# Two levels of Strassen's algorithm for the output product of a fused attention and feed-forward kernel

## The chip, the cores and the metric

The kernel runs on one core of one Trainium2 chip. The metric is the device time of one execution in microseconds (us), the median over several runs. Engines are named as in the profile: PE is the matmul engine, PEld its loading of the stationary operand, DVE the vector engine, ACT the scalar engine, POOL the GpSimd engine, SP the queue that issues most transfers.

## What is computed

Attention with a hash mask, then a feed-forward block with a quick GELU, all in float32 (the two weight matrices arrive as float64). Cut to what matters:

```python
batch, n_heads, seq, head_dim = (4, 8, 768, 64)          # attention, q k v in float32
mask = q_bucket[:, :, :, None] == k_bucket[:, :, None, :] # 6 sign bits of a projection
attn = softmax(where(mask, q @ k.T / sqrt(D), -1e9));  x = attn @ v
x = x.transpose(0, 2, 1, 3).reshape(3072, 512)            # tokens x d_model
h = x @ w_in                                              # 512 x 2048, float64 weights
g = h * (1.0 / (1.0 + np.exp(-1.702 * h)))
out = (g @ w_out).astype(np.float32)                      # 2048 x 512, float64 weights
```

## The kernel before

The attention part (up to about 334 us of the profile) leaves x transposed in on-chip memory (`xT`, model dimension on partitions, 3072 tokens along the free axis). The change does not touch it. What follows is `feed_forward`, in two stages.

**Hidden stage.** The hidden product is made by one level of Strassen's algorithm (in the variant with seven products and fifteen sums). There are 24 tasks: three blocks `sb` of 1024 tokens, and in each eight tasks `mt` of 2 x 128 hidden units. A task is a 2 x 2 block product: the two halves of the hidden units (i), the two halves of the model dimension (summed over), the two 512-token halves of the block (j). `hidden(sb, mt)` supplies the matmuls of one product: two steps of the inner dimension, 128 x 128 stationary, 512 streamed. The profile shows a float32 matmul as two instructions ("passes"), so a product is 4 passes and a task 28. `task` runs the seven products in the order 1, 6, 7, 5, 2, 3, 4 and combines them: ACT copies product 1 out of PSUM, DVE makes seven adds, each of a PSUM tile and an SBUF tile of 128 x 512. The four finished quarters go through GELU on ACT and are stored to a scratch tensor in DRAM (`g_dram`).

The sums of weight quarters that Strassen's algorithm needs are made by POOL, one task ahead, in the first token block (`in_sums`, by way of `sums_a`, lines 198 to 201). The sums of activation quarters `xT` are made by DVE, once per token block (`sums_b`, lines 206 to 209).

Behind the adds of each task, work that isn't urgent is handed out from the list `todo`: the conversion of the float64 bits of one chunk of weights to float32 (`convert`, seven DVE instructions of 512 elements, lines 171 to 186, and one on ACT; two late chunks of `w_in` in tasks 1 and 2, then 16 chunks of `w_out`), and after these the sums of quarters of `w_out` (`sums_b` on POOL, four instructions of 2048 elements).

**Output stage.** Six tasks, one per 512 tokens, again one level of Strassen's algorithm over token halves, the halves of the 2048 hidden units and the halves of the 512 model dimensions. `fetch(n)` brings the four quarters of the hidden values back from `g_dram` (four transfers of 1 MB), `g_sums` makes the sums of quarters on DVE (four instructions of 2048 elements) while the task before is running, `outputs` has the hidden values as the stationary operand (128 x 128) and the weights or their sums streamed (256): 16 matmuls per product, 32 passes. The quarters come out with tokens on partitions and are stored directly.

**Order.** The instructions of PE, DVE, ACT and POOL run in the order of the program text (`manual_schedule`), each engine its own queue, in order. The transfers of SP are ordered by a planner from its own estimate of when each becomes possible, and are issued in that order. PSUM has eight banks, used in rotation by the products, so PE can be up to eight products ahead of the engine that empties them. The tiles `u`, `v`, `c12`, `c21`, `c22` of a task have two buffers each.

Of the kernel before, what the change touches and what calls it, by code (L numbers as in the profile page):

```python
# [19 lines left out]
P = 128  # L20
# [18 lines left out]
def kernel(  # L39
# [102 lines left out]
    g_dram = dram.tile([FC, P, N], F32, name="g_dram")  # L142
# [14 lines left out]
    def convert(cv, dst, src, queue=None):  # L157
# [4 lines left out]
        def of(x):  # L162
            return x if len(dst.shape) == 2 else x.rearrange("p (j d) -> p j d", j=dst.shape[1])
# [47 lines left out]
    K2, F2, D2 = KC // 2, FF // 2, DM // 2  # L211
# [448 lines left out]
    def feed_forward(tag, late=()):  # L660

        G2 = XT // 2
        outv = out.rearrange("(s i m p) (j d) -> s i j p m d", i=2, m=G2 // P, p=P, j=2)
        n1, n2 = N // (2 * XT), N // XT
        with ExitStack() as fctx:
            stage = fctx.enter_context(tc.tile_pool(name=f"stage{tag}", bufs=2, side="right"))
            late, todo_sums = list(late), []
            sets = [fctx.enter_context(tc.tile_pool(name=f"f0{tag}", bufs=6, space=PSUM, side="right"))]
            todo, turn = [], [-1]

            def task(mm, emit, mid=(), end=(), parts=1):
                u, v, c12, c21, c22 = (stage.tile([P, XT], F32, tag=x, name=x) for x in ("u", "v", "c12", "c21", "c22"))

                def product(i):
                    turn[0] += 1
                    ps = sets[turn[0] % 8 // 6 if len(sets) > 1 else 0].tile([P, XT], F32, tag="p", name="product")
                    mm(i, ps)
                    return ps

# [5 lines left out]
                emit(1, 1, c22)  # L685
                nc.vector.tensor_tensor(c12, p, v, op=Alu.add)
                nc.vector.tensor_tensor(u, product(2), u, op=Alu.add)
                emit(0, 0, u)
# [3 lines left out]
                emit(0, 1, c12)  # L692
                p = product(4)
                for cols in (slice(i * XT // parts, (i + 1) * XT // parts) for i in range(parts)):
                    nc.vector.tensor_tensor(c21[:, cols], p[:, cols], c21[:, cols], op=Alu.add)
                    emit(1, 0, c21[:, cols], cols.start)
                for x in end:
                    x()
                if todo:
                    todo.pop(0)()  # L700


            LEFT = dict(zip(range(1, 8), (0, 1, 6, 3, 4, 5, 2)))
            RIGHT = dict(zip(range(1, 8), (0, 2, 3, 6, 4, 5, 1)))

            def hidden(sb, mt):
                wq, xq = quarters_in(slice(mt * P, (mt + 1) * P)), quarters_x(sb)

                def mm(i, ps):
                    for kc in range(K2):  # L710
                        nc.tensor.matmul(ps, wq[LEFT[i]][:, kc, :], xq[RIGHT[i]][:, kc, :],  # L711
                                         start=(kc == 0), stop=(kc == K2 - 1))

                def emit(i, j, c, _=0):
                    nc.scalar.activation(c, c, Act.Gelu_apprx_sigmoid)  # L715
                    t0 = (2 * sb + j) * XT
                    loader[0].dma_start(out=g_dram[i * (FC // 2) + mt, :, t0 : t0 + XT], in_=c)

                steps = sums_b(nc.vector, *quarters_x(sb + 1)) if mt == FC // 2 - 1 and sb + 1 < n1 else []
                return mm, emit, steps[:3], steps[3:]  # L720
# [3 lines left out]
            def g_views(n):  # L724

                if n % 2:
                    x = [w_in_sb[:, i, :].rearrange("p (c t) -> p c t", t=G2) for i in range(4)]
                    return x + [s_in[:, i].rearrange("p k (c t) -> p k c t", t=G2) for i in range(3)]
                x = [xT[:, i, 0 : 4 * XT].rearrange("p (c t) -> p c t", t=G2) for i in range(4)]
                y = [xT[:, K2 * i : K2 * (i + 1), 4 * XT : 6 * XT].rearrange("p k (c t) -> p k c t", t=G2) for i in range(2)]  # L730
                z = t_x.rearrange("p i k t -> p (i k t)")[:, 0 : FC // 2 * G2].rearrange("p (k c t) -> p k c t", k=K2, t=G2)
                return x + y + [z]

            def fetch(n):
                for x, (i, k) in zip(g_views(n), ((0, 0), (0, 1), (1, 0), (1, 1))):
                    t0 = n * XT + i * G2
                    src = g_dram[k * (FC // 2) : (k + 1) * (FC // 2), :, t0 : t0 + G2].rearrange("c p t -> p c t")
                    loader[0].dma_start(out=x, in_=src)

            def g_sums(n):  # L740
                q = g_views(n)
                return sums_a(nc.vector, *[x.rearrange("p (k c) t -> p k c t", k=K2) for x in q[:4]], *q[4:])

            def outputs(n):
                gq = g_views(n)

                def mm(i, ps):
                    ps = ps.rearrange("p (m d) -> p m d", d=D2)
                    for m in range(G2 // P):
                        for c in range(FC // 2):  # L750
                            at = LEFT[i]
                            x = gq[at][:, c] if at < 4 else gq[at][:, c // (FC // 4), c % (FC // 4)]
                            nc.tensor.matmul(ps[:, m, :], x[:, m * P : (m + 1) * P], wqs[RIGHT[i]][:, c, :],  # L753
                                             start=(c == 0), stop=(c == FC // 2 - 1))

                def emit(i, j, c, start=0):
                    c = c.rearrange("p (m d) -> p m d", d=D2)
                    m0 = start // D2
                    loader[0].dma_start(out=outv[n, i, j][:, m0 : m0 + c.shape[1], :], in_=c)

                return mm, emit
# [12 lines left out]

            for sb in range(n1):
                for mt in range(FC // 2):
                    n = sb * (FC // 2) + mt
                    if n == 1:
                        wop = fctx.enter_context(tc.tile_pool(name=f"wo{tag}", bufs=1))
                        cv = fctx.enter_context(tc.tile_pool(name=f"cv{tag}", bufs=1))  # L780
                        w_out_sb = wop.tile([P, 2, FC, D2], F32, name="w_out_sb")
                        t_out = wop.tile([P, 3, FC // 2, D2], F32, name="t_out")
                        wqs += [w_out_sb[:, j, FC // 2 * k : FC // 2 * (k + 1), :] for k in range(2) for j in range(2)]
                        wqs += [t_out[:, i] for i in range(3)]
                        steps = conversions(cv, late + [(w_out_sb[:, :, fc, :], wo[fc]) for fc in range(FC)])
                        todo += [lambda: [next(steps) for _ in range(LATE)]] * 2 if late else []
                        todo += [lambda: (next(steps), next(steps))] * FC
                        todo += sums_b(nc.gpsimd, *wqs)
# [3 lines left out]
                    if (sb, mt) == (n1 - 1, 0):  # L792
                        fetch(0)
# [4 lines left out]
                    if sb == 0 and mt + 1 < FC // 2:  # L798
                        todo_sums = in_sums(mt + 1)
# [63 lines left out]
```

## Time and profile before

| | |
|---|---|
| time, median of 3 runs | 921.9 us (921.57 to 922.57) |
| the profiled execution | 921.21 us, span 919.2 us, mean granted PE clock 0.999 |
| PE busy in the span | 909.3 us (99%) |
| DVE, ACT, POOL busy | 569.8, 301.3, 157.3 us |
| attention | to about 334 us |
| hidden stage (matmuls of line 711) | 334.1 to 623.5 us |
| output stage (matmuls of line 753) | 623.5 to 913.6 us |
| DMA traffic | 94.2 MB, mean 102 GB/s |

All times of instructions are in microseconds from the start of the span. A line of a timeline gives the start, the duration, the engine, the line of the kernel, the operation, the output and inputs by the program's names, the output's and inputs' shapes, and in brackets how long the engine was idle before it and who released it. Matmul durations include the pipeline's fill and drain, so two matmuls in a row overlap; their pace is read from the chain of waits, which counts each microsecond once. In a group's row, behind the count: busy time, mean nanoseconds of one, idle time before, and what ended it.

### The profile page before, as it was taken

The page shows a single profiled execution, that of the slowest core. Times are in us where ns is not written, and L with a number is a line of the kernel's source. Part 1 is how long each engine was busy: PE and PEld are TensorE (multiplying, and loading weights), DVE is VectorE, ACT ScalarE, POOL GpSimd, SP SyncE. Part 2 cuts the span into 40 slices and gives each one's busy share as a digit, 9 for nine tenths or more (in the row PEclk, how much of TensorE's full clock was granted, in tenths as well). Part 3 has the DMA queues.
Part 4 walks back from the last instruction along what each step waited for, and adds up shares of the span by engine and source line. Part 5 has one row for each costly group of instructions (what it writes and reads, how often), then busy time and mean ns, then how long its engine had stood idle before and what let it go on. Part 6 is the DMA issues. An engine that isn't in the chain of part 4 may idle for free.

```text
span 919.2 us, 11502 instructions
## 1 busy us (share of the span) xinstructions
PE 909.3 (99%) x4245; PEld 536.3 (58%) x4245; DVE 569.8 (62%) x766; ACT 301.3 (33%) x483; POOL 157.3 (17%) x154
## 2 busy tenths in 40 slices
PE   9999999999999999999999999999999999999997
PEld 4444444444444444444444444448888888888886
DVE  4798888888889846788877888334413223141410
ACT  5656766765676532233333232221000000000000
POOL 4232432243333270500010002300000000000000
PEclk9999999999999999999999999999999999999999
DMA  4634345434433012343333572236333324140101
GB/s 100 119 80 101 79 85 101 102 81 83 97 78 79 21 35 103 116 153 120 138 138 126 186 260 108 88 129 226 115 115 115 115 85 145 58 125 12 35 13 36
DMA packets 171503, 94.21 MB, mean 102 GB/s; under 512 B 122128, under 2 KB 155056, under 8 KB 171440
## 3 DMA queue, kind: packets, MB, share of 16 engines
q1 hardware_dynamic: 170832, 92.45, 35.3%
q10 hardware_dynamic: 608, 0.96, 0.3%
q8 instruction: 35, 0.57, 0.3%
q14 instruction: 28, 0.23, 0.1%
HBM read 60.82 MB, written 31.46 MB: 100 GB/s over the span
## 4 chain that ended last, share of the span: by engine, by line
PE 97%; DVE 1%; DMA 1%; ACTq 0%; issue 0%; SPq 0%; ACT 0%; DVEq 0%
PE product L753 32%; PE product L711 31%; PE ps L419 16%; PE av L443 13%; PE dn L462 3%; PE hash L395 1%; DMA q<-in_q_dram 0%; PE tp L353 0%; ACTq L407 0%; PE warm L346 0%; PE hash L360 0%; DVE acc L435 0%; SPq L315 0%; DMA qf<-f 0%; DVE qT L378 0%
## 5 line engine op out<-in xcount | busy, mean ns | idle before, releaser
L420 ACT ACTIVATE e<-ps 128x768 f32<-128x768 f32 x192 | 151.4, 812 | 19.2 <-PE ps L419 13.1
L419 PE MATMUL ps<-qT,kT 64*128 64x384 f32 x768 | 155.1, 482 | 0.0
L711 PE MATMUL product<-xT,w_in_sb 128*128 128x512 f32 x288 | 135.5, 593 | 0.0
L443 PE MATMUL av<-e,v 128*64 128x385 f32 x768 | 130.2, 486 | 0.9 <-ACT xT L456 0.9
L715 ACT ACTIVATE c<-c 128x512 f32<-128x512 f32 x72 | 45.2, 630 | 183.9 <-DVE c L684 133.4
L680 ACT COPY u<-product 128x512 f32<-128x512 f32 x30 | 17.2, 575 | 246.0 <-PE product L753 242.0
L443 PEld LDWEIGHTS av<-e,v 128*64 128x64 f32 x768 | 54.9, 136 | 70.6 <-issue 69.0
L711 PEld LDWEIGHTS product<-xT,w_in_sb 128*128 128x128 f32 x288 | 54.6, 190 | 68.5 <-issue 60.7
L711 PE MATMUL product<-t_x,s_in 128*128 128x512 f32 x192 | 90.2, 592 | 0.0
L419 PEld LDWEIGHTS ps<-qT,kT 64*128 64x128 f32 x768 | 68.2, 188 | 35.5 <-issue 35.5
L427 POOL TENSOR_TENSOR acc<-e 128x768 f32<-128x768 f32 x32 | 49.3, 1542 | 208.1 <-DVE acc L435 139.6
L681 DVE TENSOR_TENSOR v<-product,u 128x512 f32<-128x512 f32 x30 | 20.6, 686 | 88.4 <-PE product L753 72.3
L419 PE MATMUL ps<-qf,kf 64*128 64x384 bf16 x384 | 63.0, 324 | 0.7 <-ACT e L420 0.6
L753 PE MATMUL product<-w_out_sb,xT 128*128 128x256 f32 x288 | 63.6, 379 | 0.0
L753 PE MATMUL product<-t_out,xT 128*128 128x256 f32 x288 | 63.6, 379 | 0.0
L753 PE MATMUL product<-w_out_sb,w_in_sb 128*128 128x256 f32 x288 | 63.6, 379 | 0.0
L711 PEld LDWEIGHTS product<-t_x,s_in 128*128 128x128 f32 x192 | 36.5, 190 | 45.9 <-issue 45.7
L753 PEld LDWEIGHTS product<-w_out_sb,xT 128*128 128x128 f32 x288 | 54.7, 190 | 7.9 <-issue 0.5
L753 PEld LDWEIGHTS product<-t_out,xT 128*128 128x128 f32 x288 | 54.7, 190 | 7.4
L753 PEld LDWEIGHTS product<-w_out_sb,w_in_sb 128*128 128x128 f32 x288 | 54.7, 190 | 7.4
L428 POOL TENSOR_TENSOR acc<-acc,e 128x768 f32<-128x768 f32 x32 | 56.7, 1773 | 2.5
L684 DVE TENSOR_TENSOR c<-product,c 128x512 f32<-128x512 f32 x30 | 20.7, 691 | 45.1 <-PE product L753 37.3
(127 smaller groups left out, 1125.9 us busy)
## 6 DMA issues: line engine op xcount, KB each, us to landing
g_dram<-c SPq DMA_DIRECT2D x72, 256.0 KB
xT<-g_dram SPq DMA_DIRECT2D x12, 1024.0 KB
w_in_sb<-g_dram SPq DMA_DIRECT2D x12, 1024.0 KB
raw<-in_moe_w_out_dram SPq DMA_DIRECT2D x16, 512.0 KB
raw<-in_moe_w_in_dram SPq DMA_DIRECT2D x15, 512.0 KB
v<-in_v_dram SPq DMA_DIRECT2D x32, 192.0 KB
g_dram<-u SPq DMA_DIRECT2D x24, 256.0 KB
k<-in_k_dram SPq DMA_DIRECT2D x60, 96.0 KB
```

The source lines that it names most:

```text
L419: nc.tensor.matmul(ps[:, j, 0:HS], a[hs, keys], m[hs, cols], start=not last, stop=last)
L420: nc.scalar.activation(es[c][:, kt, :, 0:HS], ps[:, :, 0:HS], Act.Exp, scale=1.0 / D**0.5)
L427: nc.gpsimd.tensor_tensor(acc, es[c][:, 0, :, 0:HS], es[c][:, 1, :, 0:HS], op=Alu.add)
L428: nc.gpsimd.tensor_tensor(acc, acc, es[c][:, 2, :, 0:HS], op=Alu.add)
L443: nc.tensor.matmul(av[D * j : D * (j + 1), :], vt[:, t, j, :], es[c][:, t, j, :], start=(t == 0), stop=(t == T - 1))
L462: nc.tensor.matmul(dn[D * j : D * (j + 1), :], ones, acc[:, j, :], start=True, stop=True)
L680: nc.scalar.copy(u, product(1))
L681: nc.vector.tensor_tensor(v, product(6), u, op=Alu.add)
L684: nc.vector.tensor_tensor(c22, p, c21, op=Alu.add)
L711: nc.tensor.matmul(ps, wq[LEFT[i]][:, kc, :], xq[RIGHT[i]][:, kc, :], start=(kc == 0), stop=(kc == K2 - 1))
L715: nc.scalar.activation(c, c, Act.Gelu_apprx_sigmoid)
L753: nc.tensor.matmul(ps[:, m, :], x[:, m * P : (m + 1) * P], wqs[RIGHT[i]][:, c, :], start=(c == 0), stop=(c == FC // 2 - 1))
```

## The change

The output product gets a second level: two levels of Strassen's algorithm in place of one.

- The hidden stage's task (now inside `hidden`) no longer stores only the four quarters of the hidden values. As soon as the quarters of a task have gone through GELU, POOL makes the four first-level sums of them (`sums_b` on POOL, 128 x 512 each, two of the results in place), and all seven first-level operands that the outer products need are stored to `g_dram`, whose layout now has partitions in front and rows of 2 KB per task. `in_sums` of the next task stand ahead of a task on POOL instead of behind it.
- The output stage has 21 steps: three token blocks of 1024, times seven outer products in the order 1, 6, 7, 5, 2, 3, 4. A step is again a Strassen product with seven inner products (order 1, 2, 3, 6, 7, 5, 4). Now the weights are the stationary operand (128 x 128) and the hidden values are streamed (256 tokens): an inner product is four matmuls.
- Before a step, its first-level operand is fetched in two transfers of 1 MB into one of two buffers, one step ahead, and DVE makes its four second-level sums (`sums_b`, 1024 elements). The first-level sums of `w_out` are made by DVE (2048 elements, behind tasks 21 and 22), the second-level ones by POOL (`sums_a`, 512 elements: four for the first step behind task 22, then four in each of the first six steps).
- The result of an outer product is accumulated while the inner products are combined: most steps add the four quarters of an earlier outer product, in SBUF, on DVE.
- Results have the model dimension on partitions. DVE turns them by 32 x 32 transposes (`turned`, four of 256 elements for each outer quarter), and they are stored in rows of 512 bytes (`written`).
- The conversion writes the columns of `w_out` split by their remainder modulo 4, a strided write.

The diff, cut:

```diff
-    g_dram = dram.tile([FC, P, N], F32, name="g_dram")
+    g_dram = dram.tile([7 * (N // 1024), P, FC // 2, 512], F32, name="g_dram")
...
-            return x if len(dst.shape) == 2 else x.rearrange("p (j d) -> p j d", j=dst.shape[1])
+            return x if len(dst.shape) == 2 else x.rearrange("p (x r) -> p x r", r=dst.shape[2])
...
+            def hidden(sb, mt, mid=(), end=()):
                 u, v, c12, c21, c22 = (stage.tile([P, XT], F32, tag=x, name=x) for x in ("u", "v", "c12", "c21", "c22"))
+                t2, t4 = (stage.tile([P, XT], F32, tag=x, name=x, bufs=1) for x in ("t2", "t4"))
...
+                def keep(at, x):
+                    loader[0].dma_start(out=g_dram[len(LEFT) * sb + at, :, mt, :], in_=x)
+
+                def emit(c, at=None):
+                    nc.scalar.activation(c, c, Act.Gelu_apprx_sigmoid)
+                    if at is not None:
+                        keep(at, c)
...
+                for f, kept in zip(sums_b(nc.gpsimd, u, c12, c21, c22, v, t2, t4), ((4, v), (1, c12), (5, t2), (6, t4))):
+                    f()
+                    keep(*kept)
                 for x in end:
                     x()
...
+            steps_out = [(sb, o) for sb in range(n1) for o in OUTER]
+            raw_g = [None, s_in[:, 0:2].rearrange("p i k f -> p (i k f)").rearrange("p (c t) -> p c t", t=XT)]
             def fetch(n):
+                sb, o = steps_out[n]
+                for h in range(2):
+                    cs = slice(h * F4, (h + 1) * F4)
+                    loader[0].dma_start(out=raw_g[n % 2][:, cs], in_=g_dram[len(LEFT) * sb + RIGHT[o], :, cs, :])
...
             def g_sums(n):
+                return sums_b(nc.vector, *g_quarters(n)) if n < len(steps_out) else [lambda: None] * 4
...
+            def product_of_halves(n, acc, after):
...
+                def product(i):
+                    ps = bank()[:, 0:TH]
+                    for c in range(F4):
+                        nc.tensor.matmul(ps, wq[LEFT[i]][:, c, :], gq[RIGHT[i]][:, c, :], start=(c == 0), stop=(c == F4 - 1))
+                    return ps
...
+                nc.scalar.copy(u, product(1))
+                add(c11, product(2), u)
+                if acc is not None:
+                    add(c11, c11, acc[:, 0])
+                nc.scalar.copy(c12, product(3))
+                after(0)
+                add(v, product(6), u)
+                add(c21, product(7), v)
+                if acc is not None:
+                    add(v, v, acc[:, 1])
+                    add(c22, c21, acc[:, 3])
+                    add(c21, c21, acc[:, 2])
+                add(c12, c12, v)
+                after(1)
+                p = product(5)
+                add(c22, p, c21 if acc is None else c22)
+                add(c12, p, c12)
+                after(2)
+                add(c21, product(4), c21)
+                after(3)
...
-                        todo += [lambda: (next(steps), next(steps))] * FC
-                        todo += sums_b(nc.gpsimd, *wqs)
+                        places = [w_out_sb[:, :, fc, :].rearrange("p r x -> p x r") for fc in range(FC)]
+                        steps = conversions(cv, late + [(places[fc], wo[fc]) for fc in range(FC)])
+                        free = [i for i in range(LATE + 1, 3 * MT) if i % MT != MT - 1]
+                        for i in (list(range(1, LATE + 1)) if late else []) + free[:FC]:
+                            todo[i] = [lambda: next(steps)] * 2
+                        w_steps = sums_a(nc.vector, *wqs)
+                        todo[3 * MT - 3], todo[3 * MT - 2] = w_steps[:2], w_steps[2:] + sums_a(nc.gpsimd, *w_quarters(OUTER[0]))
...
+                    if n == 3 * MT - 3:
+                        cv_ctx.close()
+                        gp = fctx.enter_context(tc.tile_pool(name=f"gp{tag}", bufs=1))
+                        raw_g[0] = gp.tile([P, FC // 2, XT], F32, name="raw_g")
                         fetch(0)
+                    if sb == 0 and mt + 1 < MT:
+                        for f in in_sums(mt + 1):
+                            f()
...
+            for n, (sb, o) in enumerate(steps_out):
...
+                    fetch(n + 1)
+                if n + 1 < len(OUTER):
+                    for f in sums_a(nc.gpsimd, *w_quarters(OUTER[n + 1])):
                         f()
+                later_sums = g_sums(n + 1)
...
+                acc = {6: 1, 7: 6, 2: 1, 3: 6, 4: 7}.get(o)
+                ms[o] = product_of_halves(n, None if acc is None else ms[acc], after)
```

## The prediction

> **What bounds the kernel now.** I read the page first: busy time of each engine, then the chain that ended last.
>
> ```profile
> PE 909.3 (99%) x4245; PEld 536.3 (58%) x4245; DVE 569.8 (62%) x766; ACT 301.3 (33%) x483; POOL 157.3 (17%) x154
> ...
> PE 97%; DVE 1%; DMA 1%; ACTq 0%; issue 0%; SPq 0%; ACT 0%; DVEq 0%
> ```
>
> Then the same chain in order of time (start, us, what):
>
> ```profile
> 346.94 276.58 PE product L711 x644
> ...
> 623.52 290.09 PE product L753 x1344
> ...
> 913.63 0.43 DVE c L695
> ```
>
> PE has no gap. A hidden pass costs (12.02 + 276.58)/672 = 0.4295 us, so a task of 28 passes 12.03. An output pass costs 290.09/1344 = 0.2158. Anything taken from PE shortens the run, as long as DVE, POOL and the DMAs keep up; so the next view is the timeline of DVE. One hidden task with a weight conversion, POOL idle:
>
> ```profile
> 419.88 0.68 DVE L171 SCALAR_TENSOR_TENSOR sign<-raw,mask 128x512 uint32<-128x512 uint32 x1
> ...
> 424.18 0.69 DVE L186 SCALAR_TENSOR_TENSOR w_out_sb<-size,w_out_sb 128x512 f32<-128x512 f32 x1
> 424.79 0.68 DVE L681 TENSOR_TENSOR v<-product,u 128x512 f32<-128x512 f32 x1
> ```
>
> Seven conversion steps take 424.79 - 419.88 = 4.91 us. The seven adds behind them start 0.77, 0.78 and then 0.61 apart: 4.58. DVE needs 9.49 of 12.03; it has 2.54 to spare. Now the one task in which POOL worked at the same time, DVE and then POOL:
>
> ```profile
> 383.83 1.09 DVE L171 SCALAR_TENSOR_TENSOR sign<-raw,mask 128x512 uint32<-128x512 uint32 x1
> 384.84 1.22 DVE L172 SCALAR_TENSOR_TENSOR bits<-raw,mask_7fffffff 128x512 uint32<-128x512 uint32 x1
> 386.09 1.10 DVE L174 TENSOR_TENSOR bits<-bits,sign 128x512 uint32<-128x512 uint32 x1
> ...
> 391.64 0.68 DVE L681 TENSOR_TENSOR v<-product,u 128x512 f32<-128x512 f32 x1
> ```
>
> ```profile
> 382.84 0.72 POOL L198 TENSOR_TENSOR s_in<-w_in_sb 128x256 f32<-128x256 f32 x1
> ...
> 384.33 1.18 POOL L200 TENSOR_TENSOR s_in<-s_in,w_in_sb 128x256 f32<-128x256 f32 x1
> 385.59 1.05 POOL L201 TENSOR_TENSOR s_in<-w_in_sb,s_in 128x256 f32<-128x256 f32 x1
> ```
>
> The same seven steps took 391.64 - 383.83 = 7.81 us, and POOL's sums rose from 0.72 to 1.05-1.18: the two engines take turns, a pair every 1.13 instead of 0.72 us of DVE. One such meeting costs DVE 0.41. It hits DVE instructions with both inputs in SBUF. The product adds, with one input in PSUM, kept 0.68-0.69 from 376.72 to 383.22 while POOL summed at 0.72. Nothing is lost there today, since the spare 2.54 covers it. This is what the change leans on.
>
> **PE, removed.** Outputs go from 6 x 7 x 16 matmuls to 3 x 7 x 7 x 4 = 588, of the same shape (128 columns loaded, 256 streamed), two passes each: 1176 passes at 0.2158 = 253.8 us. That is 290.1 - 253.8 = 36.3 us less, all of it on the path. A step (one outer product, 56 passes) lasts 12.09.
>
> **POOL, added in the hidden stage.** Each of 24 tasks gets four 128x512 sums. The trace has no such size; its neighbours are
>
> ```profile
> L427 POOL TENSOR_TENSOR acc<-e 128x768 f32<-128x768 f32 x32 | 49.3, 1542 | 208.1 <-DVE acc L435 139.6 <-ACT e L420 63.6 <-DVE rt L476 4.9
> L206 POOL TENSOR_TENSOR t_out<-w_out_sb 128x2048 f32<-128x2048 f32 x1 | 4.5, 4531 | 81.9 <-DVE w_out_sb L186 81.9
> ```
>
> and 0.72 for 256. A line through 256 and 2048, which are sums of the same two helpers, gives 1.26 us; one through 256 and 768 gives 1.13. I take 1.26, the helper being the same, and keep both. Four make 5.0 us of a 12-us task, so POOL itself keeps up. But the sums become possible when the last GELUs of a task end, and that is when DVE starts its conversion. They will meet. A 512-wide sum is 0.54 longer than a 256-wide one, so a meeting costs DVE 0.41 + 0.54 = 0.95 (by 1.13: 0.82).
>
> DVE per conversion task is then 9.49 + 4 x 0.95 = 13.29, which is 1.26 over the 12.03 of PE. Twelve tasks of the second and third token blocks: 15.1. In the first block POOL also makes the weight sums (0.72 each) right behind, and two of these meet the last two conversion steps: 14.11, 2.08 over; six tasks: 12.5. Hidden loss 27.6 us (by 1.13: 12 x 0.74 + 6 x 1.56 = 18.3). Eight PSUM banks let PE run ahead of DVE, so I expect it not evenly but in lumps: product 6 of tasks 8 and 16 waits for activation sums that DVE makes behind its backlog, and the first output steps inherit the rest. Tasks without a conversion (7, 15, 21, 22, 23) have other two-input sums of about the same length (1.22 for 1024, 2.28 for 2048) and about break even; the four 2048-wide weight sums that move from POOL to DVE lie there.
>
> The Trainium skill (SBUF — State Buffer, § Who interferes with whom) has a rule against this change: a DVE instruction with two SBUF inputs and a GpSimd instruction that reads SBUF exclude each other, and the later one is blocked until the first has finished. Taken literally, a meeting would cost the whole 1.26 and the sum would be some 30 us longer, about 959; the pair above (1.13, not 0.72 + 0.72) says that part of each instruction lies outside the lock, and the row decides.
>
> **Outputs, DVE and POOL.** A step with an accumulation has eleven adds of 256 (0.42 us by the 128x256 form of L695, started 0.34 to 0.50 apart: 4.2) and four sums of 1024 (1.19 each: 4.8): 9.0 of 12.09, nine of the fifteen with two SBUF inputs. POOL's 24 weight sums of 512 wait only for the end of the hidden stage, so they queue at once, 24 x 1.29 = 31 us, over the first three or four steps. If 85% of them meet DVE: 24 x 0.95 x 0.85 = 19.4, less the spare 3 us of 3.5 steps (10.5): 9 us lost (by 1.13: 6.2). Bounds 0 (none meet) and 12.3 (all do).
>
> After that, transposes: 0.58 for 384 and 0.94 for 768 give 0.46 for 256, 1.8 per group, so 10.8 in a step; 13.2 in the one after outer product 5, whose 1.1 us over is held by the banks and its neighbours' spare. Cost nothing; if they took twice that, some 2 us per step in question.
>
> **DMAs.** Hidden: seven stores of 256 KB plus one load of 512 KB per 13 us, 180 GB/s; the window 500-600 moved 158 at a share of 0.45. Outputs: 2 MB per step plus 6.3 MB of results, 198 GB/s; 620-640 moved 268 at 0.82. A fetch is issued a step ahead, and its target is free after product 7 of the step before: up to about 14 us are hidden, after that each microsecond counts 20 times. I price it at nothing. If that cover were gone, DVE's sums for the next step would wait, and behind them the adds of products 5 and 4; PE would stop once its eight banks are full. SP issues 8 instead of 5 transfers per task, in order; three now wait for POOL, and the ACT copy and adds of the task after next wait for these stores (two buffers each, so some 12 us of cover for a POOL sum and a store). The conversion's last three steps now write with a stride; the nearest row, L171 reading every second word, takes 0.68 as the others do, so I add nothing (at most as much again, 0.7 x 3 per task, which would be another 30 us and is left to the tail above the range).
>
> **Clock.** No gap of more than 1.2 us on PE is in the trace; the lumps would be 7 to 9 us. At the start, after idling, PE was slower:
>
> ```profile
> 3.81 2.89 PE L353 MATMUL tp<-ident,k 128*64 128x128 f32 x24
> 6.39 1.65 PE L353 MATMUL tp<-ident,q 128*64 128x128 f32 x24
> ```
>
> The same 24 transposes cost 1.24 more. Three lumps: 0 to 3.7; I take 3. The Trainium skill (TensorE: Matmul & The Clock Gate, § Why this matters for your kernels) warns of gaps beyond about 3 us, and its window of 3.4 us at half rate would make it an estimated 5.
>
> **End.** Behind the last product come one more transpose (0.46) and four stores on two queues instead of two: one more issue (0.37) and 256 KB more (0.7 at the 355 GB/s of the fetches), less the 0.2 of the second half-add. +1.3.
>
> **Sum.** Against the profiled execution (921.2; span 919.2 and 2.0 around it): 921.2 - 36.3 + 27.6 + 9 + 1.3 + 3 = 925.8. The median of the runs is 0.7 higher: **926.5**.
>
> **Rivals.**
> - *POOL is quicker* (913): 1.13 per sum. 921.9 - 36.3 + 18.3 + 6.2 + 1.3 + 1.5 (smaller lumps). For it: the 768-wide row. Against: the slope of the helpers' own rows. The sign turns at about 1.22.
> - *They hardly meet* (887): 921.9 - 36.3 + 1.3. It needs POOL's sums to miss the conversions; but both are released by the same add.
> - *Conversion loads come late* (945): today a raw load is issued within 0.1 us of the step that frees its buffer. Behind stores that wait for POOL on SP it can slip. There are about 4 us to spare; each microsecond beyond that costs 16. At 1.1 beyond: 926.5 + 18.
> - That the matmuls don't get fewer is excluded by the count.
>
> **How the numbers follow.** Main case 0.55 (own range 919-934), quicker POOL 0.23, hardly meeting 0.07, late loads 0.15. A change of under 0.2% (1.8 us) can't be told from none. Faster: 0.03 of the main case + 0.22 + 0.07 = 0.32. Same: 0.06 + 0.01 = 0.07. Slower: 0.61. The range 906-945 leaves out 887, the low end of the quicker POOL and the far half of the late loads, 0.17.
>
> **What would show it.** Right: 1176 passes on the outputs' line at 0.216; POOL's 512-wide sums at 1.26 alone and 1.6 or more beside conversions; conversion steps at 1.6-1.7 in all conversion tasks; PE gaps before product 6 of tasks 8 and 16, released by DVE. Wrong: conversions still 4.9 us per task; POOL sums under 1.2; gaps released by a DMA, or gaps in steps 7 to 20.

## The result: 3.5% slower, and 28 us beyond the forecast

The changed kernel takes 954.07 us (median of 4 runs, 953.72 to 956.44) beside 922.2 us of the kernel before: ratio 1.0352, 95% interval 1.0334 to 1.0370. Slower was forecast at 0.61, but by 4.6 us, not by 32; the range ended at 945. The profiled execution has a span of 951.8 us.

Busy time of the engines and the chain that ended last, from the page of the changed kernel:

```profile
PE 890.9 (94%) x4077; PEld 509.6 (54%) x4077; DVE 805.4 (85%) x1048; ACT 312.4 (33%) x519; POOL 348.5 (37%) x274
...
PE 61%; DVE 27%; issue 6%; POOL 4%; DMA 1%; ACTq 0%; DVEq 0%; SPq 0%; ACT 0%; POOLq 0%
```

PE executes 4245 - 4077 = 168 matmul instructions fewer, as counted, but it no longer carries the chain alone: 27% of it are DVE, and more than half of that share are the conversion steps (L172 to L184). Who PE waits for from 330 us on (total, number, longest):

```profile
PE product L690 <- DVE t_x L209: 19.2, 2, 10.4
PE product L690 <- DVE v L703: 10.3, 7, 2.3
PE product L690 <- POOL s_in L201: 5.6, 3, 2.9
PE product L792 <- POOL xT L202: 5.2, 1, 5.2
PE product L792 <- DVE t2g L209: 3.6, 1, 3.6
PE product L792 <- DVE t2b L209: 2.6, 1, 2.6
```

None of PE's waits is for a DMA. The two waits for `t_x` stand before product 6 of tasks 8 and 16 (450.45 and 567.56 us), where the forecast put them. One conversion of the second token block, the seven steps on DVE and then POOL's four sums beside them (lines are one or more further down than before):

```profile
492.18 0.68 DVE L172 SCALAR_TENSOR_TENSOR sign<-raw,mask 128x512 uint32<-128x512 uint32 x1
492.78 1.77 DVE L173 SCALAR_TENSOR_TENSOR bits<-raw,mask_7fffffff 128x512 uint32<-128x512 uint32 x1
494.59 1.64 DVE L175 TENSOR_TENSOR bits<-bits,sign 128x512 uint32<-128x512 uint32 x1
496.26 1.64 DVE L178 TENSOR_TENSOR sign<-bits,mask_ff 128x512 uint32<-128x512 uint32 x1
497.93 2.01 DVE L182 SCALAR_TENSOR_TENSOR w_out_sb<-raw,sign 128x512 f32<-128x512 uint32 x1
499.98 1.05 DVE L184 TENSOR_TENSOR w_out_sb<-bits,w_out_sb 128x512 f32<-128x512 f32 x1
501.14 1.06 DVE L187 SCALAR_TENSOR_TENSOR w_out_sb<-size,w_out_sb 128x512 f32<-128x512 f32 x1
502.10 0.68 DVE L703 TENSOR_TENSOR v<-product,u 128x512 f32<-128x512 f32 x1
```

```profile
492.40 1.60 POOL L207 TENSOR_TENSOR v<-c,u 128x512 f32<-128x512 f32 x1 [7.99 <-ACT c L698]
494.08 1.59 POOL L208 TENSOR_TENSOR c<-c,c 128x512 f32<-128x512 f32 x1
495.64 1.71 POOL L209 TENSOR_TENSOR t<-c,v 128x512 f32<-128x512 f32 x1
497.43 1.60 POOL L210 TENSOR_TENSOR t<-c,t 128x512 f32<-128x512 f32 x1
```

All four sums meet conversion steps, and the two steps in the middle take 1.64 instead of 0.69: the forecast 0.95 per meeting, to the digit. But the last two steps meet nothing and still take 1.05. The seven steps last 502.10 - 492.18 = 9.92 us; 4.91 + 4 x 0.95 = 8.71 was forecast.

Set against the steps of the forecast (span and its parts, us):

| | forecast | before | after | measured |
|---|---|---|---|---|
| start of the outputs | +27.6 | 623.5 | 670.9 | +47.4 |
| outputs, to the last matmul | -36.3 + 9 = -27.3 | 290.1 | 270.9 | -19.2 |
| last matmul to the end | +1.3 | 5.6 | 10.0 | +4.4 |
| clock | +3 | | | inside the others |
| sum | +4.6 | 919.2 | 951.8 | +32.6 |

### The profile page after: what moved, and what is told of

It is laid out like the page before. It is cut to its first block, busy times and chain, and to the rows that moved or that the text cites. A ratio compares the mean times of both kernels' runs of the same rounds, so it can differ in the third digit from the quotient of the medians.

```text
span 951.8 us, 11992 instructions
## 1 busy us (share of the span) xinstructions
PE 890.9 (94%) x4077; PEld 509.6 (54%) x4077; DVE 805.4 (85%) x1048; ACT 312.4 (33%) x519; POOL 348.5 (37%) x274
## 4 chain that ended last, share of the span: by engine, by line
PE 61%; DVE 27%; issue 6%; POOL 4%; DMA 1%; ACTq 0%; DVEq 0%; SPq 0%; ACT 0%; POOLq 0%
PE product L792 23%; PE ps L420 15%; PE av L444 13%; PE product L690 5%; DVE bits L173 3%; DVE sign L178 3%; DVE bits L175 3%; DVE w_out_sb L182 3%; PE dn L463 3%; DVE w_out_sb L184 2%; DVE xT L796 2%; DVE sign L172 1%; DVE c L704 1%; DVE v L703 1%; DVE c L715 1%
## 5 line engine op out<-in xcount | busy, mean ns | idle before, releaser
L690 PE MATMUL product<-xT,w_in_sb 128*128 128x512 f32 x288 | 138.4, 603 | 10.3 <-DVE v L703 10.3
L690 PE MATMUL product<-t_x,s_in 128*128 128x512 f32 x192 | 97.0, 630 | 25.0 <-DVE t_x L209 19.2
L207 POOL TENSOR_TENSOR v<-c,u 128x512 f32<-128x512 f32 x24 | 41.8, 1741 | 156.1 <-ACT c L698 156.1
L798 ACT COPY u<-product 128x256 f32<-128x256 f32 x21 | 7.8, 371 | 176.1 <-PE product L792 131.8
L792 PE MATMUL product<-raw_g,w_out_sb 128*128 128x256 f32 x192 | 45.3, 387 | 0.0
L690 PE MATMUL product<-t_x,w_in_sb 128*128 128x512 f32 x96 | 45.1, 592 | 0.0
L690 PE MATMUL product<-xT,s_in 128*128 128x512 f32 x96 | 45.1, 592 | 0.0
L420 PEld LDWEIGHTS <-kf 64*128 64x128 bf16 x384 | 18.9, 94 | 42.2 <-issue 20.7
L173 DVE SCALAR_TENSOR_TENSOR bits<-raw,mask_7fffffff 128x512 uint32<-128x512 uint32 x32 | 41.4, 1293 | 0.0
L208 POOL TENSOR_TENSOR c<-c,c 128x512 f32<-128x512 f32 x24 | 40.2, 1675 | 1.9
L792 PEld LDWEIGHTS product<-raw_g,w_out_sb 128*128 128x128 f32 x192 | 37.5, 195 | 5.9 <-DVE c L706 0.2
```

The costliest lines, as they stand in the source:

```text
L173: nc.vector.scalar_tensor_tensor(bits, hi, 3, masks[0x7FFFFFFF], op0=Alu.logical_shift_left, op1=Alu.bitwise_and)
L207: return [lambda: eng.tensor_tensor(t1, b12, b11, op=Alu.subtract), lambda: eng.tensor_tensor(b12, b22, b12, op=Alu.subtract), lambda: eng ...
L208: lambda: eng.tensor_tensor(b12, b22, b12, op=Alu.subtract),
L420: nc.tensor.matmul(ps[:, j, 0:HS], a[hs, keys], m[hs, cols], start=not last, stop=last)
L792: nc.tensor.matmul(ps, wq[LEFT[i]][:, c, :], gq[RIGHT[i]][:, c, :], start=(c == 0), stop=(c == F4 - 1))
```

## The experiments

Each was compared with the kernel before on the same chip (921.4 to 921.7 us). Theory: PE waits because POOL's sums and DVE's conversions exclude each other in part, and because the strided conversion costs DVE more than nothing.

### What POOL's sums cost

**e3_nosums**: POOL's activation sums left out; the same tiles are stored unsummed, so the outputs are other numbers, with the same transfers.

```diff
-                t2, t4 = (stage.tile([P, XT], F32, tag=x, name=x, bufs=1) for x in ("t2", "t4"))
...
-                for f, kept in zip(sums_b(nc.gpsimd, u, c12, c21, c22, v, t2, t4), ((4, v), (1, c12), (5, t2), (6, t4))):
-                    f()
+                for kept in ((4, u), (1, c12), (5, c22), (6, c21)):
                     keep(*kept)
```

> Leaves out POOL's four first-level sums of hidden values in all 24 tasks and stores other tiles of the same size in their place, so that all transfers stay (the output is therefore not the reference's). Theory 'meetings': with nothing to meet, a conversion task is 9.5 + 1.1 = 10.6 of 12.03 on DVE, the hidden stage falls from 336.6 to about 289.4 and the time to 900 to 908. Rival 'transfers': the seven stores per task, not the sums, are what is late; 945 to 954.

Measured: 897.65 us (896.94 to 898.13), ratio 0.9743 (0.9727 to 0.9759). PE has no gap at all in the hidden stage, although the conversion's last steps still take 1.08. So neither strides nor transfers stop PE by themselves there; POOL's sums are the condition for the loss in the hidden stage. (In the outputs PE still waits 5.5 us for `t2g`.)

**e2_mid**: the same work, but the conversion steps are handed out behind the add of product 2 instead of behind the last add.

```diff
-                    hidden(sb, mt, x[:3], x[3:] + todo.pop(n, []) + (g_sums(0) if n == 3 * MT - 1 else []))
+                    t = todo.pop(n, [])
+                    early, behind = (t, []) if n < 3 * MT - 3 else ([], t)
+                    hidden(sb, mt, x[:3] + early, x[3:] + behind + (g_sums(0) if n == 3 * MT - 1 else []))
```

> The seven conversion steps of a task stand in the middle of the task (behind the add of product 2) instead of at its end; DVE's and POOL's instructions are the same ones, the strided write stays. Theory 'meetings': at the end of a task the conversions and POOL's four sums are released by the same add and take turns; in the middle POOL has nearly finished. Conversion steps return to 0.7 (the three strided ones 1.07), a task needs about 9.5 + 1.1 + at most 1 = 11.6 of 12.03 on DVE, the long PE gaps and the slow passes behind them go: 905 to 920. Rival 'volume': DVE simply has too much to do, or stores and loads are late; then moving the same work gains little, 945 to 954.

Measured: 916.46 us (915.55 to 917.5), ratio 0.9943 (0.9926 to 0.9959): nothing is removed, 38 us are gained, and instead of 3.5% slower the change is 0.6% faster than the kernel before. The same steps in the middle of a task, on DVE, and ahead of them one product add beside two of POOL's sums:

```profile
487.15 0.69 DVE L706 TENSOR_TENSOR c<-product,c 128x512 f32<-128x512 f32 x1
```

```profile
485.33 1.27 POOL L208 TENSOR_TENSOR c<-c,c 128x512 f32<-128x512 f32 x1
486.56 1.27 POOL L209 TENSOR_TENSOR t<-c,v 128x512 f32<-128x512 f32 x1
```

```profile
489.65 0.68 DVE L173 SCALAR_TENSOR_TENSOR bits<-raw,mask_7fffffff 128x512 uint32<-128x512 uint32 x1
490.37 0.69 DVE L175 TENSOR_TENSOR bits<-bits,sign 128x512 uint32<-128x512 uint32 x1
491.09 0.69 DVE L178 TENSOR_TENSOR sign<-bits,mask_ff 128x512 uint32<-128x512 uint32 x1
491.82 1.06 DVE L182 SCALAR_TENSOR_TENSOR w_out_sb<-raw,sign 128x512 f32<-128x512 uint32 x1
```

POOL now sums beside the product adds, which read PSUM: sums 1.27, adds 0.69, neither delayed. What is left is the first conversion step, which often still meets the last sum (L172 takes 1.03 in the mean of 18, here 0.78). So what costs is when the two meet, not how much either does. The strided step stays at 1.06.

**e5_sumdve**: the sums stay where they are in the order, but DVE makes them (`sums_b(nc.vector, ...)` for `sums_b(nc.gpsimd, ...)`).

> The changed kernel with one edit: the four first-level activation sums of every hidden task are made by DVE instead of POOL, same order, same stores. DVE gets 24 x 4 x 0.69 = 66 us of work that it did not have, POOL loses it. Theory 'meetings': beside the conversions a 512-wide POOL sum costs DVE 0.95 us, more than the 0.69 it takes to make that sum itself, so a conversion task gets shorter by about 4 x 0.26 = 1.0 us and the weight sums of the first block no longer stand behind activation sums on POOL; the tasks without a conversion and the start of the outputs give some of it back. About 944 us (938 to 950), conversion steps back at 0.69 and 1.06 us outside the first block. Rival 'volume': DVE is simply short of time and what POOL takes off it is a gain; then 66 us more on an engine that already holds PE back cost 25 us or more: 975 us and above.

Measured: 940.73 us (938.93 to 941.8), ratio 1.0209 (1.0192 to 1.0227). DVE takes over 66 us of work and the run is 13 us shorter: where every sum meets a DVE instruction, POOL's help costs DVE more (0.95) than the sum itself (0.72 to 0.75 in the mean here).

### What the stride costs

**e1_contiguous**: the conversion writes contiguously, and reads its inputs with the stride instead.

```diff
-            return x if len(dst.shape) == 2 else x.rearrange("p (x r) -> p x r", r=dst.shape[2])
+            return x if len(dst.shape) == 2 else x.rearrange("p (x r) -> p r x", r=dst.shape[1])
...
-                        places = [w_out_sb[:, :, fc, :].rearrange("p r x -> p x r") for fc in range(FC)]
+                        places = [w_out_sb[:, :, fc, :] for fc in range(FC)]
```

> The three last steps of a weight conversion write contiguous runs of 128 and read their inputs with a stride instead; nothing else differs from the changed kernel (954.1 us). Theory 'stride': in the trace of the changed kernel these steps take 1.05 to 1.07 us each without POOL, against 0.69 before, and under the lock that excess is added in full: 16 chunks x 3 x 0.37 = 18 us of DVE. They should fall to 0.69 to 0.72 alone, and the time to about 935 (930 to 940). Rival 'any stride': a strided read costs DVE as much as a strided write; 950 to 954. Rival 'meetings only': the stride is not what counts, because PE waits for meetings with POOL; less than 5 us gained.

Measured: 956.73 us (955.59 to 957.51), ratio 1.0381 (1.0364 to 1.0398). The last two steps take 1.14 and 1.11 in the mean, before this edit 1.11 and 1.11: a strided read costs what a strided write costs. **e4_both** (this edit and that of e2_mid):

> Both: conversions in the middle of the task, and written contiguously. Theory: DVE has 9.5 to 10.5 of 12.03 per task, the hidden stage is back at 289 to 293, the output stage keeps POOL's burst of weight sums in its first steps (8 to 12 us over 253.8), the end costs 2 more: 899 to 907. By the rival 'volume' 930 to 954.

Measured: 918.59 us (916.68 to 921.74), ratio 0.9971 (0.9960 to 0.9983). A miss that follows from the one before: with nothing saved by the order of reads and writes, it is e2_mid again.

**e6_onestride**: two of the three steps work in a contiguous scratch tile, only the last writes the strided place.

```diff
-        nc.vector.scalar_tensor_tensor(dst, of(lo), 2.0**-52, of(sign.bitcast(F32)), op0=Alu.mult, op1=Alu.mult)
+        low = dst if len(dst.shape) == 2 else cv.tile([P, CW], F32, tag="low", name="low")
+        nc.vector.scalar_tensor_tensor(low, lo, 2.0**-52, sign.bitcast(F32), op0=Alu.mult, op1=Alu.mult)
...
-        nc.vector.tensor_tensor(dst, of(bits.bitcast(F32)), dst, op=Alu.add)
+        nc.vector.tensor_tensor(low, bits.bitcast(F32), low, op=Alu.add)
...
-        nc.vector.scalar_tensor_tensor(dst, of(size), (1.125 * 2.0**-15) ** 2, dst, op0=Alu.is_ge, op1=Alu.mult)
+        nc.vector.scalar_tensor_tensor(dst, of(size), (1.125 * 2.0**-15) ** 2, of(low), op0=Alu.is_ge, op1=Alu.mult)
```

> The changed kernel with one edit: the two steps that multiply and add in the conversion of w_out work in a contiguous scratch tile, and only the last step writes the strided place. Theory 'stride': each of the three strided steps costs 0.37 us more than a contiguous one (1.06 against 0.69), whatever else goes on; two of the three become contiguous, 16 chunks x 2 x 0.37 = 12 us less DVE time where DVE holds PE back: about 942 us (936 to 946), the two steps at 0.69 alone. Rival: the 0.37 is not the stride but hidden time of waiting for POOL or for the instruction before, so the steps stay above 0.9 and the time stays within 3 us of 954.

Measured: 944.45 us (943.21 to 946.1), ratio 1.0246 (1.0225 to 1.0266): 9.6 us for two of three.

**e11_nostride**: no stride at all.

```diff
-                        places = [w_out_sb[:, :, fc, :].rearrange("p r x -> p x r") for fc in range(FC)]
+                        places = [w_out_sb[:, :, fc, :] for fc in range(FC)]
```

> The changed kernel, but the conversion of w_out writes the columns in four contiguous blocks of 128 instead of by their remainder modulo 4; the weights land in the wrong columns, so the columns of the result come out permuted, while all sizes, engines and transfers are the same. It sizes the term that the prediction set to nothing. Theory: the three steps take 0.69 instead of 1.06 us, 16 x 3 x 0.37 = 17.8 us of DVE gone; two of the three gave 9.6 us of the run's time, so three give 14: about 940 us (936 to 943), and the 13 us to the predicted 926.5 lie elsewhere (the clock behind the gaps, POOL's late weight sums, the tail). Rival: the strides explain the whole miss, then 926 to 930 us.

Measured: 938.66 us (937.87 to 939.48), ratio 1.0187 (1.0170 to 1.0204): the strides make 15.4 of the 27.6 us by which the forecast was missed. The outputs now start at 651.8 us instead of 670.9. The forecast, which had no strides in it, said 623.5 + 27.6 = 651.1.

**e12_ahead**: e11_nostride, with POOL's weight sums of the first block further ahead.

```diff
-                    if sb == 0 and mt + 1 < MT:
-                        for f in in_sums(mt + 1):
-                            f()
+                    if sb == 0:
+                        for m in {0: (1, 2, 3), 3: (4, 5), 4: (6,), 5: (7,)}.get(mt, ()):
+                            for f in in_sums(m):
+                                f()
```

> e11_nostride (columns of the result permuted) with one more edit: POOL makes the weight sums of tasks 1 to 3 before task 0 and the others before tasks 3 to 5, so that none stands behind activation sums in the first token block. Theory: the 5.6 us that PE waits there for POOL go, and some slow passes behind them; DVE's surplus of the first block (two more meetings per task) goes too: 6 to 10 us less than e11_nostride, about 932 us (928 to 936). Rival: PE's lead of eight banks hides POOL's lateness from DVE's and the two are one queue, so the wait only changes its name: within 3 us of e11_nostride.

Measured: 938.29 us (936.91 to 938.74), ratio 1.0178 (1.0161 to 1.0195). The rival held. PE's waits from 330 us on, in e11_nostride and then in e12_ahead:

```profile
PE product L690 <- DVE t_x L209: 17.1, 2, 9.4
...
PE product L690 <- POOL s_in L201: 2.4, 3, 1.9
PE product L690 <- DVE v L703: 1.2, 1, 1.2
```

```profile
PE product L690 <- DVE t_x L209: 18.8, 2, 9.4
...
PE product L690 <- DVE v L703: 3.0, 3, 1.2
```

The wait for POOL (2.4 us) is gone, and DVE's have grown by 3.5. While DVE is the longer queue, a wait removed elsewhere only changes its name.

### The stride and the clock by themselves

**e9_probe**: the kernel before, with additions that nobody uses on DVE in the tenth and the thirteenth task.

```diff
+                if tasks[0] == 10:
+                    for _ in range(4):
+                        add(room[:, 0:512], a[:, 0:512], b[:, 0:512])
+                    for _ in range(4):
+                        add(room[:, 0:1024:2], a[:, 0:512], b[:, 0:512])
...
+                if tasks[0] == 13:
+                    for _ in range(18):
+                        add(room[:, 512:1024], a[:, 0:512], b[:, 0:512])
```

> The kernel before, with DVE instructions added that nobody uses, while POOL is idle: behind the adds of task 9 (the tenth) 32 additions of 512 float32, four of each of eight shapes (contiguous; written to every 2nd, 4th, 8th word; written in runs of 4 words 6 KB apart, like the conversion of w_out; one input read at every 2nd, every 4th word; both inputs at every 4th), and behind task 12 18 contiguous ones. Theory 'stride': DVE pays from 16 bytes of distance on, 0.69 us for contiguous and every 2nd word, 1.05 for every 4th and beyond and for the far runs; rival: every stride costs, 1.05 for every 2nd word too. Theory 'clock': the 28 us of additions exceed what eight PSUM banks hold (13.7 us), PE stands still for 10 to 17 us, and its next passes take 0.6 to 0.9 us instead of 0.43 although POOL does nothing, 2 to 3 us lost beyond the gap itself; rival: the slow passes behind the gaps of the changed kernel come from POOL's accesses, then the passes here are back at 0.43 at once. Time 922 + gaps of 10 to 20 + 3 = 939 us (932 to 948).

Measured: 951.98 us (951.29 to 952.58), ratio 1.0331 (1.0313 to 1.0348). The additions by shape (ns: least, median, most): contiguous; every 2nd and every 4th word written; one input at every 2nd and at every 4th word:

```profile
L680 DVE TENSOR_TENSOR t_out<-xT x4: 682/691/694, 460.8 to 462.9; 128x512 f32<-128x512 f32 x4
L680 DVE TENSOR_TENSOR t_out<-xT x4: 692/692/693, 463.7 to 465.8; 128x512 f32<-128x512 f32 x4
L680 DVE TENSOR_TENSOR t_out<-xT x4: 1075/1080/1095, 466.6 to 469.9; 128x512 f32<-128x512 f32 x4
```

```profile
L680 DVE TENSOR_TENSOR t_out<-xT x4: 691/691/691, 479.8 to 481.9; 128x512 f32<-128x512 f32 x4
L680 DVE TENSOR_TENSOR t_out<-xT x4: 1054/1056/1058, 482.7 to 485.9; 128x512 f32<-128x512 f32 x4
```

A step of two words is free, one of four costs 0.37 to 0.39 us more per 512 elements, on either side. It costs no more beyond: every 8th word written 1.08, words 6 KB apart (much as the conversion writes them) 1.03, both inputs at every 4th 1.06.

PE in the same run, around the two stalls:

```profile
492.03 3.40 PE L744 MATMUL product<-xT,w_in_sb 128*128 128x512 f32 x4 [21.35 <-DVE v L713]
495.26 1.88 PE L744 MATMUL product<-t_x,s_in 128*128 128x512 f32 x4
```

```profile
533.52 3.78 PE L744 MATMUL product<-xT,w_in_sb 128*128 128x512 f32 x4 [3.77 <-DVE v L713]
537.10 2.97 PE L744 MATMUL product<-t_x,s_in 128*128 128x512 f32 x4
539.91 1.88 PE L744 MATMUL product<-xT,w_in_sb 128*128 128x512 f32 x4
```

The time missed the expectation (939) because PE stood still longer, 25.1 us in the two stalls: it stopped 9.9 us after the additions began, not 13.7, since the conversion steps ahead of them (4.9 us) had already used up part of its lead of eight banks. 25.1 and the slow passes make 29.6 of the 30.3 us.

Four passes normally last 1.88. After a gap of 21.35 us they lose 3.40 - 1.88 = 1.5; after one of only 3.77 they lose 1.9 + 1.1 = 3.0. Around the first stall POOL is idle, so the slow passes behind it are not POOL's; in the windows of 5 us between 475 and 490 us the granted clock is 0.50. Behind the second stall POOL is making a sum of `w_out` (533.09 to 537.63), so there only the granted clock tells: 0.75 from 530 to 535 us and 0.57 from 535 to 540.

### Versions that beat both kernels

**e7_tuned**: e2_mid with the edits of e6_onestride and e12_ahead.

> Three edits to the changed kernel: the conversions in the middle of the task (as in e2_mid), only one strided step per chunk (as in e6_onestride), and POOL's weight sums of the first token block made earlier (those of tasks 1 to 3 before task 0, the others before tasks 3 to 5) so that none stands behind activation sums. Theory: what is left in e2_mid (916.5) is 8 us of strided steps in the hidden stage, 5.9 us of gaps that PE spends on POOL's late weight sums, and the gaps of the first output steps: about 906 us (902 to 910). Rival: the weight sums made in one heap meet DVE's adds and conversions at the start of the stage and cost there what they save; then 911 us or more.

Measured: 910.18 us (907.94 to 910.66), ratio 0.9868 (0.9848 to 0.9888), just beyond the far end of the expectation. The waits for POOL's weight sums in the first block are gone here; the outputs keep theirs.

**e8_tuned_dve**: the second-level weight sums of the six output steps on DVE as well.

```diff
-                    for f in sums_a(nc.gpsimd, *w_quarters(OUTER[n + 1])):
+                    for f in sums_a(nc.vector, *w_quarters(OUTER[n + 1])):
```

> e7_tuned with one more edit: the 24 second-level sums of output weights in the first six output steps (512 wide) are made by DVE instead of POOL. Theory 'meetings': each costs DVE 0.69 instead of up to 0.95 for meeting it on POOL, and the product that needs it no longer waits for a queue on POOL: 4 to 6 us less than e7_tuned, about 901 us (898 to 905). Rival: they don't all meet, so DVE's 16.6 us more in six steps is a net loss: e7_tuned plus 3 us or more.

Measured: 900.19 us (899.34 to 900.96), ratio 0.9766 (0.9749 to 0.9782). Ten us, twice the estimate. Without POOL, DVE's 1024-wide sums take 1.21 to 1.23 from the second step on (up to 2.29 in e7_tuned), and no product in the outputs waits for POOL.

**e10_sooner**: in tasks 7 and 15, the first and third activation sum of the next block stand right behind the adds of product 5, the second behind the add of product 2.

> e8_tuned_dve with one edit: in tasks 7 and 15 the first and third sum of the activations of the next token block stand right behind the adds of product 5 instead of product 2, and the second behind them. Theory: product 6 of the next block waits for the third sum (3.9 us in e8_tuned_dve, with slow passes behind it); it comes 1.8 us sooner, which saves 2 to 3 us: about 898 us (896 to 899.5). Rival: what is brought forward delays the adds behind it and PE waits for a bank instead; no change within 1 us of 900.2.

Measured: 898.14 us (897.99 to 898.44), ratio 0.9745 (0.9729 to 0.9762). PE's waits in the two stages, all that are left (the line left out belongs to the attention):

```profile
PE product L691 <- DVE t_x L210: 2.8, 1, 2.8
PE product L795 <- DVE t2g L210: 2.2, 2, 1.2
...
PE product L795 <- DVE t2b L210: 0.6, 1, 0.6
PE product L795 <- issue: 0.5, 1, 0.5
```

24 us below the kernel before. The change's arithmetic was worth having; its order of work was not.

## Why the prediction was right in kind and wrong in size

**PE, removed: right.** From 729.20 us on the chain holds 209.18 us of matmuls for 968 passes, 0.2161 each.

**POOL's sums: right.** 1.27 alone (forecast 1.26, the rival 1.13), 1.59 to 1.71 beside conversions; 0.95 per meeting. "POOL is quicker" and "they hardly meet" fall with that. The direction was not luck: without the strides the change is still slower (938.66 us), and where the meetings are moved or left out it is not (916.46, 897.65).

**The strided writes: the step that failed.** The term was set to nothing because L171, reading every second word, takes 0.68. The row was real and the nearest, and on the other side of an edge that lies between two and four words. Three steps cost 3 x 0.37 = 1.1 us per task: PE's waits in the second block repeat every 14.56 us (517.40 and 531.96), so a task takes 2.5 us more than PE's 12.03, twice the forecast 1.26. e11_nostride puts it at 15.4 us of the run. The prediction named the risk, bounded it at another 30 us, and left that outside the range: the failure is one of the range as well as of the term.

The Trainium skill (SBUF — State Buffer, § Door 1: The DMA port swizzle) speaks of lines of 16 bytes, of which at least two accesses must fall into the same line for full bandwidth. e9_probe agrees: two words per line 0.69, one word 1.08. Taken up, that sentence would have stood against the row of L171. The same place gives "4 fp32" as how far one can stride for free; every 4th word was not free here, every 2nd was.

**The clock and the gaps: mis-sized, mostly through the strides.** Hidden stage: 47.4 us, of which the waits explain 19.2 + 10.3 + 5.6 = 35.1; of the other 12.3 an estimated 8.4 are passes at half the clock (half of the 16.8 us in which PE works between a gap and the clock's rise). Forecast were three lumps and 3 us; there were twelve gaps. Without the strides, with the surplus that was forecast, PE stops less often: e11_nostride has six gaps of 20.7 us together, most of it the two lumps before `t_x`, and its hidden stage is 28.3 us longer than before, where 27.6 and 3 for the clock were forecast. The row that priced a lump, 1.24 us at the start of the kernel, was no reading of the clock: the granted clock of the kernel before is 1.00 there, in every window of 1 us from 3 to 7.

The granted clock shows what a gap's price depends on. In the changed kernel, read in windows of 1 us, it falls to 0.50 at 413.6, 444.3, 533.1, 560.4, 649.1, 679.8 and 710.6 us and is back at 1.00 at 417.0, 454.6, 536.5, 570.6, 652.5, 683.3 and 717.4. All these times are whole numbers of steps of 3.413 us from the first, within 0.02 us. The clock falls at the end of a step in which PE stood still for 2.27 us or more, never after one with 1.91 or less; it rises at the end of a step with 0.58 or less. So two gaps of 2.28 us differ by where they lie: the one before 517.40 lies across the end of a step, the one before 531.96 lies whole within one. The five windows are such steps; the granted clock (PEclk) is the third number from the right:

```profile
core 0: us, PE busy (x) PEld busy (x) DVE busy (x) ACT busy (x) POOL busy (x), PEclk, DMA share, GB/s
512.60:516.01 3.41, 2.52 (x6) 0.76 (x4) 3.27 (x3) 0.00 (x0) 1.00 (x1) 1.00 0.51 175
516.01:519.43 3.42, 2.02 (x5) 1.06 (x6) 3.13 (x5) 0.32 (x1) 0.00 (x0) 1.00 0.34 132
529.67:533.08 3.41, 1.13 (x4) 0.64 (x4) 3.01 (x5) 0.00 (x0) 0.00 (x0) 1.00 0.56 162
533.08:536.49 3.41, 3.41 (x6) 1.35 (x5) 3.41 (x6) 2.29 (x4) 0.37 (x1) 0.50 0.27 99
536.49:539.90 3.41, 3.41 (x9) 1.49 (x9) 3.38 (x3) 1.24 (x3) 3.33 (x3) 1.00 0.35 132
```

The Trainium skill (TensorE: Matmul & The Clock Gate, § What's actually happening) describes a free-running window of some 3.4 us in which the clock falls or rises. The traces agree: the steps above are such windows, and in e9_probe the clock falls at 474.4 and 532.5 us and rises at 494.9 and 539.3, which are 17 steps between the falls, and 6 and 2 from a fall to its rise. By that window's half rate a gap would cost an estimated 1.7. Measured were 1.5 us after the gap of 21.35, where PE restarted 2.9 us before the rise, and 3.0 after that of 3.77, where it restarted 5.8 us before it.

**The outputs: mis-sized.** Forecast 9 us over 253.8, measured 270.9 - 253.8 = 17.1. The forecast counted what DVE loses; it didn't follow the chain DVE, POOL, PE at the seam. POOL's sums for the first step, then DVE's:

```profile
673.15 2.13 POOL L200 TENSOR_TENSOR w_out_sb<-w_out_sb 128x512 f32<-128x512 f32 x1
675.24 2.24 POOL L201 TENSOR_TENSOR xT<-xT,w_out_sb 128x512 f32<-128x512 f32 x1
677.56 2.12 POOL L202 TENSOR_TENSOR xT<-w_out_sb,xT 128x512 f32<-128x512 f32 x1
```

```profile
674.19 2.17 DVE L208 TENSOR_TENSOR raw_g<-raw_g 128x1024 f32<-128x1024 f32 x1
676.28 2.28 DVE L209 TENSOR_TENSOR t2g<-raw_g,t 128x1024 f32<-128x1024 f32 x1
```

Beside 1024-wide sums of DVE a 512-wide POOL sum takes 2.1 to 2.2, and PE waits 5.2 us for the last of them. The queue on POOL was late already: in tasks 21 and 22 two of its four sums took 3.18 to 3.21 beside DVE's 2048-wide ones. Steps 7 to 20 have no gap, as forecast; e8_tuned_dve shows what the burst was worth in the tuned kernel, 10 us. Without the strides the outputs are still 20.4 us over 253.8, so that of what is then left of the miss (938.7 - 926.5 = 12.2) nearly all lies here and at the end.

**The end: mis-sized.** +4.4 instead of +1.3: from DVE's last instruction to the end 8.3 us pass (943.5 to 951.8), before 4.8 (914.4 to 919.2). By the trace it is mostly issue: SP is done with the last store 3.7 us behind DVE's last instruction (947.2), before 0.5 (914.9); from there to the end 4.6 us pass, before 4.3.

**Right without cost:** the transposes took 0.63 instead of the estimated 0.46 and stopped nobody. "Conversion loads come late" falls: in the two stages neither PE nor DVE waits for a DMA.

**The literal lock rule.** The rule that the prediction took from the Trainium skill (SBUF — State Buffer, § Who interferes with whom) would have made the sum 959, near the 954 measured, by accident: a pair takes 1.66 here, not 0.69 + 1.27 = 1.96. The missing us were the strides, the seam before the outputs and the end.

## What to carry to other kernels

Before work goes to POOL, look at what DVE does at that moment: beside DVE instructions with two SBUF inputs the help can cost more than it takes over, beside adds from PSUM it is free, so move one of the two in time before you move it to another engine. An access pattern that the trace doesn't show is not priced by its nearest neighbour if an edge may lie between; put both ends into the range. And when an engine is over the pace of the bottleneck in every period, count a gap for each period in which the lead of the banks no longer covers it, not a few lumps, and a clock penalty for each gap that fills most of one of the clock's steps: of the twelve gaps here five had one.

## What the hardware showed unexpectedly

- DVE, float32, 512 elements: a step of 8 bytes between words costs nothing, one of 16 bytes makes 0.69 into 1.06 to 1.08 us, read or written, and larger steps, tried on the write, cost no more.
- The clock after a gap: it changes only at the ends of steps of 3.413 us that run on through the whole trace. A gap of 1.95 us that lies within one step halves it (e11_nostride: PE restarts at 411.72, the clock falls at 412.1), one of 2.28 that lies across two doesn't (517.40 in the changed kernel). Behind a gap it cost 1.5 us (gap of 21.35) or 3.0 (gap of 3.77), by how far the rise was off.
- A pair of instructions that exclude each other: 1.64 to 1.66 us for 0.69 and 1.27, so about 0.3 of the two overlap; for 0.72 and 0.72 it was 1.13.
